# Placing the sign of a float64 weight with the scaling instruction on ScalarE instead of a bitwise instruction on VectorE

## The chip, the cores and the metric

The kernel runs on one core of a Trainium2 chip. The metric is the device time of one execution in microseconds (us); three runs of the kernel before gave 1048.39, 1048.4 and 1048.1, median 1048.39. The engines are named as in the profile: PE (TensorE matrix products), PEld (its weight loads), DVE (VectorE), ACT (ScalarE), POOL (GpSimd) and SP (SyncE, which issues all DMAs here; SPq is its queue).

## The reference

Three parts run one after the other on 2304 rows. The weights (`moe_w_*`, `moe2_w_*`) arrive as float64, everything else as float32.

```python
# q, k, v: (4, 8, 576, 64); average over groups of 4 rows, full attention on the averages
out_up = repeat(softmax(scale * q_d @ k_d.T) @ v_d, 4)
# banded attention: key within 3 rows of the query
out_local = softmax(where(|i - j| < 4, scale * q @ k.T, -1e9)) @ v
x = (out_up + out_local)                      # -> (2304, 512)
x = (silu(x @ w_gate) * (x @ w_val)) @ w_out  # 512 -> 1536 -> 512
h = x @ w_in                                  # 512 -> 2048
return (max(h, 0) + alpha * min(h, 0)) @ w_out2
```

## The kernel before

**Products.** Each float32 operand is held as a high and a low part, and each product is three PE instructions (high*high, high*low, low*high: lines 464 to 466 and 601 to 603). So each weight has to be turned from float64 into two such parts before PE can use it.

**Weights.** The five weight matrices are cut into 68 pieces. `w_load` (lines 99 to 108) brings a piece into a slot as raw 32-bit word pairs, 128 partitions by 512 weights (512 KB). `w_split` (lines 121 to 134) turns it into the two parts, which then take the slot:

- line 126, ACT: the high word, read as a float32, times 2^-112, into a working tile `st`;
- line 127, DVE: `st` shifted left by 3 bits;
- line 128, DVE: the sign bit of the high word is masked out and OR-ed into `st`;
- line 130, DVE: the top 3 bits of the low word are OR-ed into `st`, which is now the float32 weight;
- line 133, ACT: the high part, a rounded copy;
- line 134, POOL (DVE for half of the 32 pieces of the last part): the low part, `st` minus the high part.

36 pieces (lines 493 to 495, `prep1`) belong to the gated layer and are split at the start; 32 (lines 554 to 556, `prep2`) belong to the last layer and are split while the gated layer's last block and the last layer's first block run.

**Stages.** The attention of the first two 288-row blocks (8 head pairs) runs first, its tiles lying in slots that later weights take, so that the loads of these weights wait for it. Then the gated layer runs over 8 blocks of 288 rows by 12 pieces of 128 hidden columns (functions `m_g`, `m_v`, `m_y`: gate product, value product, output product), with the attention of the later blocks spread between them. Block 0 needs pieces 0 to 11 of each of the three matrices, and splits them as it goes. The last layer (`m2_h`, `m2_o`) runs over 5 blocks by 16 pieces.

**Order.** The program is written for a tiling framework that adds the semaphores and lets a planner with its own simulated costs and times decide in which order each engine's instructions are issued; a cost that changes can thus move other instructions in the queues. A few splits at the start are held behind attention steps on POOL by hand (`gP` in line 19, lines 485 to 491).

Of the kernel before, what the change touches and what calls it, by code (L numbers as in the profile page):

```python
# [8 lines left out]
F32 = mybir.dt.float32  # L9
F32R = mybir.dt.float32r  # L10
I32 = mybir.dt.int32
AF = mybir.ActivationFunctionType
ALU = mybir.AluOpType
AX = mybir.AxisListType
PSUM = bass.MemoryType.PSUM
DRAM = bass.MemoryType.DRAM
# [6 lines left out]
def attn_moe_moe2_kernel(  # L23
# [13 lines left out]
    nc = tc.nc  # L37
    B, H, S, D = q.shape
# [19 lines left out]
    scale = 1.0 / float(D) ** 0.5  # L58
    NEG = -1.0e9 / scale

# [1 line left out]
    wp = ctx.enter_context(tc.tile_pool(name="wp", bufs=1))  # L62
    dp = ctx.enter_context(tc.tile_pool(name="dp", bufs=1, space=DRAM))
    pp = ctx.enter_context(tc.tile_pool(name="pp", bufs=1, space=PSUM))
# [9 lines left out]
    mask = wp.tile([128, 4, SWIN], F32, name="mask")  # L74
# [7 lines left out]
    def f32(t):  # L82
        return t.bitcast(F32)

# [1 line left out]
    # A float64 word pair (H, L) becomes float32 bits: H * 2^-112 rebases the exponent, << 3 aligns it,  # L86
    # the sign comes from H and the last three mantissa bits from L. The float32 is then split exactly
    # into a 12-bit high part and a 12-bit low part.
    wsrc = {"g": w_gate.bitcast(I32), "v": w_val.bitcast(I32), "o": w_out.bitcast(I32),
            "i2": w2_in.bitcast(I32), "o2": w2_out.bitcast(I32)}  # L90

# [20 lines left out]
    def st_tile():  # L112
        c = stc[0]
        stc[0] += 1
        if c >= 3 * NEARLY:
            return stp[0].tile([128, 512], F32, tag="st", name="st", bufs=stn[0])
        if c % 2 == 0:
            stc[1] = wp.tile([128, 2, 512], F32, tag=st_slots[c // 2 % len(st_slots)], name="st2")
        return stc[1][:, c % 2]

    def w_split(slot, eng):
        t = raw.pop(slot)
        st = st_tile()
        sti = st.bitcast(I32)
        hw, lw = t[:, :, 1], t[:, :, 0]
        nc.scalar.mul(out=st, in_=hw.bitcast(F32), mul=2.0 ** -112)
        nc.vector.tensor_scalar(out=sti, in0=sti, scalar1=3, scalar2=None, op0=ALU.logical_shift_left)
        nc.vector.scalar_tensor_tensor(out=sti, in0=hw, scalar=-2 ** 31, in1=sti,  # L128
                                       op0=ALU.bitwise_and, op1=ALU.bitwise_or)
        nc.vector.scalar_tensor_tensor(out=sti, in0=lw, scalar=29, in1=sti,  # L130
                                       op0=ALU.logical_shift_right, op1=ALU.bitwise_or)
        w = W[slot] = wp.tile([128, 2, 512], F32R, tag=slot, name="w")
        nc.scalar.copy(out=w[:, 0], in_=st)  # L133
        eng.tensor_sub(w[:, 1], st, f32(w[:, 0]))  # L134

# [1 line left out]
    hu = {}  # L137
    kTs = {}
    pbd = {}
# [5 lines left out]
    def coords(n):  # L145
        blk, hp = divmod(n, NP)
        b, half = divmod(blk, 2)
        return b, half, hp, blk
# [11 lines left out]
    def at_(n, shape, tag):  # L160
        return wp.tile(shape, F32, tag=pslot[tag, n], name=tag)

    def small(n):
        # working tiles of one head pair: parts of a weight slot at first, the pool's after that
        d = hu[n]
        if n < NPRO:
            t = at_(n, [128, 1024], "qs")
            d["qT"] = t[:, 0:HB + 8]
            d["pt"] = t[:72, 0:4 * QD].rearrange("p (h x) -> p h x", h=2)
            o = HB + 8  # L170
            d["sm"] = t[:, o:o + 2 * SW].rearrange("p (h x) -> p h x", h=2)
            d["xf"] = t[:, o:o + HB]
            o += 2 * SW
            d["qd"] = t[:, o:o + QD]
            d["up"] = t[:, o + QD:o + 2 * QD]
        else:
            d["qT"] = ap_.tile([128, HB + 8], F32, tag="qT", name="qT", bufs=1)
            d["qd"] = ap_.tile([128, QD], F32, tag="qd", name="qd", bufs=1)
# [6 lines left out]
    def a_load(n):  # L185
        b, half, hp, blk = coords(n)
        h0, t0 = 2 * hp, half * HB
        d = hu[n] = {}
        if n >= NPRO:
            # 32 x 32 blocks for the transposing copy: partition 32 i + r, column 32 m + c is row 32 m + r, column 32 i + c  # L190
            loads = [("qn", q, HB, t0)]
            if half == 0:
                loads.insert(0, ("kn", k, S, 0))
            for tag, src, rn, r0 in loads:
                t = d[tag] = ap_.tile([128, rn], F32, tag=tag, name=tag, bufs=1)
                for i in range(4):
                    nc.sync.dma_start(
                        out=t[32 * i:32 * (i + 1)].rearrange("r (m c) -> r m c", c=32),
                        in_=src[b, h0 + i // 2, r0:r0 + rn, 32 * (i % 2):32 * (i % 2 + 1)].rearrange("(m r) c -> r m c", r=32))
            return  # L200
        if half == 0:
            kn = d["kn"] = at_(n, [QB, 6, 2, D], "kn")
            for h in range(2):
                nc.sync.dma_start(out=kn[:, :, h], in_=k[b, h0 + h].rearrange("(r p) c -> p r c", p=QB))
        t = at_(n, [128, 2 * NW * 2 * D], "qv").rearrange("p (a w h c) -> p a w h c", a=2, w=NW, h=2)
        d["vw"] = t[:, 1]
        qn = d["qn"] = t[:QB, 0]
        for h in range(2):
            nc.sync.dma_start(out=qn[:, :, h], in_=q[b, h0 + h, t0:t0 + HB, :].rearrange("(r p) c -> p r c", p=QB))
# [16 lines left out]
                nc.sync.dma_start(out=vf, in_=v[b, h0:h0 + 2, f * HB:(f + 1) * HB].rearrange("h (p r) c -> p h (r c)", r=4))  # L226

    def a_load_w(n):
        # v rows of the 32-key window of each 24-query tile; rows outside the sequence meet a zero weight
        b, half, hp, blk = coords(n)  # L230
        if n < NP:
            pbd[n] = at_(n, [128, 2, NW, 128], "bd")
            (nc.vector if K["bdV"] else nc.gpsimd).memset(pbd[n], 0.0)
        if n >= NPRO:
            hu[n]["vw"] = ap_.tile([128, NW, 2, D], F32, tag="vw", name="vw", bufs=NVW)
        t = hu[n]["vw"]
        for h in range(2):
            w0 = ((b * H + 2 * hp + h) * 2 + half) * NW * 128
            nc.sync.dma_start(out=t[:, :, h], in_=vwin[w0:w0 + NW * 128, :].rearrange("(w p) c -> p w c", p=128))

    def stage(b):
        # DRAM copy of v in overlapping windows: window g holds rows 24 g - 3 .. 24 g + 28; rows outside v meet a zero weight
        nw = H * S // SUB
        g0, g1, ng = b * nw, (b + 1) * nw, B * nw

        def win(a, e):
            n = (e - a) * SWIN
            nc.sync.dma_start(
                out=vwin[a * SWIN:e * SWIN, :].rearrange("(g r) c -> g (r c)", r=SWIN),
                in_=bass.AP(v.tensor, v.offset + (a * SUB - 3) * D, [[SUB * D, e - a], [1, SWIN * D]]))  # L250

        vf = v.rearrange("b h s c -> (b h s) c")
        if g0 == 0:
            nc.sync.dma_start(out=vwin[0:3, :], in_=vf[0:3, :])
            nc.sync.dma_start(out=vwin[3:SWIN, :], in_=vf[0:SWIN - 3, :])
            win(1, 16)
            g0 = 16
        if g1 == ng:
            win(g0, g1 - 16)
            win(g1 - 16, g1 - 1)  # L260
            r0, m = (g1 - 1) * SWIN, SUB + 3
            nc.sync.dma_start(out=vwin[r0:r0 + m, :], in_=vf[B * H * S - m:, :])
            nc.sync.dma_start(out=vwin[r0 + m:r0 + SWIN, :], in_=vf[0:SWIN - m, :])
        else:
            win(g0, g1)
# [193 lines left out]
                        hp_.tile([128, KD, HB], F32R, tag="xl", name="xl"))  # L459
        return xts[blk]  # L460

# [1 line left out]
    def mm3(o, lhi, llo, rhi, rlo, first, last):  # L463
        nc.tensor.matmul(o, lhi, rhi, start=first, stop=False)  # L464
        nc.tensor.matmul(o, lhi, rlo, start=False, stop=False)  # L465
        nc.tensor.matmul(o, llo, rhi, start=False, stop=last)  # L466
# [10 lines left out]
    gates = {}  # L477

    def gate(n, stage):
        # the last instruction traced so far on each engine  # L480
        bb = tc.nc.cur_bb.bb.instructions
        for key, eng in (("D", nc.vector), ("P", nc.gpsimd), ("A", nc.scalar)):
            gates[key, n, stage] = next(i for i in reversed(bb) if i.engine == eng.engine)
# [51 lines left out]
                    out=y1[e * 128:(e + n) * 128, blk * HB:(blk + 1) * HB].rearrange("(e p) t -> p e t", p=128),  # L535
                    in_=ys.unsqueeze(1) if n == 1 else ys)

# [1 line left out]
    blocks2 = [512, 512, 512, 512, 256]  # L539
    starts2 = [sum(blocks2[:i]) for i in range(len(blocks2))]  # L540
    HT = []
# [75 lines left out]
        r0 = starts2[i] + m * 128  # L617
        nc.sync.dma_start(out=out[r0:r0 + 128, :], in_=os_)

# [1 line left out]
    if True:  # L621
        make_identity(nc, ident)
        for tok in K["lo"]:
# [11 lines left out]
        for t in srs:  # L635
            nc.vector.memset(t, 1.0)

        # mask[32 i + r, :, j]: key window j of query r of tile i; 0 <= j - r <= 6, cut at both ends of the sequence
        tmp = ap_.tile([SWIN, 4, NS, SWIN], F32, tag="vd", name="tmp", bufs=NVD)
        nc.gpsimd.memset(tmp, 0.0)  # L640
        nc.gpsimd.affine_select(out=tmp, in_=tmp, pattern=[[0, 4], [0, NS], [1, SWIN]], compare_op=ALU.is_ge, fill=NEG,
# [90 lines left out]
        for n in range(NPRO, NHU):  # L732
            if n < 2 * NP:
                c = K["c"]
# [56 lines left out]
        for t in range(len(f2s)):  # L791
            if True:
                i, j = f2s[t]
# [8 lines left out]
            if SK <= t < len(f2s):  # L802
                i, j = f2s[t - SK]
# [32 lines left out]
```

## Time and profile before

| | |
|---|---|
| time, median of 3 runs | 1048.39 us (1048.1 to 1048.4) |
| profiled execution, first to last instruction (span) | 1047.0 us |
| profiled execution's own time | not listed apart from its span; the median lies 1.4 us above the span |
| PE busy | 978.3 us (93%) |
| DVE busy | 557.9 us (53%) |
| POOL busy | 401.7 us (38%) |
| ACT busy | 292.2 us (28%) |

These are shares of the whole span. The page also cuts the span into 40 slices of 26 us; PE's digits there are 5368779 followed by nines, and DVE's are 4899997 at the start, 4 to 6 in the middle, 99972 behind it and 2 to 3 to the end. The stages therefore differ, and are read apart: the rows below come from the stretches 28 to 172 us (the 36 splits of the gated layer), 172 to 580 us, 580 to 700 us (the 32 splits of the last layer) and 700 us to the end.

### The profile page before, as it was taken

Reading aid. Unit: us, or ns where it says so; the run is one execution under the profiler, and the core shown is the slowest. Engines: PE = TensorE matmul, PEld = TensorE weight load, DVE = VectorE, ACT = ScalarE, POOL = GpSimd, SP = SyncE. Lnnn points to the kernel's source line nnn. Section 1 sums busy time; section 2 is a strip of 40 time slices with the busy share of each in tenths; the row PEclk is TensorE's granted clock in tenths of the full one; section 3 lists DMA queues with packets and bytes.
Section 4 is the critical chain, followed back from the end, with each engine's and each line's share of the span. In section 5 each row is a group of like instructions: output and inputs, shape, how many; then the busy total and the mean of one; then the engine's idle time right before and its main releaser. Section 6 shows DMA issues by size and latency. Waiting matters only on the chain.

```text
span 1047.0 us, 19294 instructions
## 1 busy us (share of the span) xinstructions
PE 978.3 (93%) x7760; PEld 872.4 (83%) x7760; DVE 557.9 (53%) x1113; ACT 292.2 (28%) x660; POOL 401.7 (38%) x492
## 2 busy tenths in 40 slices
PE   5368779999999999999999999999999999999998
PEld 4257668999999999999999998778888888888887
DVE  4899997546544555545451699972222322232232
ACT  3545443222222222222223445432111201111111
POOL 5666676223432234322224344653222322322222
PEclk9989879999999999999999999999999999999999
DMA  8995463114221132111101884200100200010010
GB/s 207 282 308 185 122 146 82 28 26 89 47 58 19 35 72 49 26 45 21 44 17 41 263 261 154 72 1 20 61 1 1 71 1 1 11 41 0 1 41 21
DMA packets 135895, 77.82 MB, mean 74 GB/s; under 512 B 97407, under 2 KB 127103, under 8 KB 135039
## 3 DMA queue, kind: packets, MB, share of 16 engines
q1 hardware_dynamic: 135804, 76.58, 26.4%
q8 instruction: 61, 1.00, 0.4%
q14 instruction: 30, 0.24, 0.1%
HBM read 67.12 MB, written 15.73 MB: 79 GB/s over the span
## 4 chain that ended last, share of the span: by engine, by line
PE 72%; DVE 12%; SPq 5%; DMA 3%; issue 3%; POOL 2%; ACT 2%; DVEq 0%; ACTq 0%; POOLq 0%
PE y L603 6%; PE y L601 6%; PE y L602 6%; PE g L464 5%; PE v L465 5%; PE v L464 5%; PE g L465 5%; PE g L466 5%; PE v L466 5%; PE y L464 4%; PE y L466 4%; PE y L465 4%; DVE st L128 3%; PE h L464 3%; PE h L466 3%
## 5 line engine op out<-in xcount | busy, mean ns | idle before, releaser
L589 POOL TENSOR_TENSOR gl<-t,gh 128x512 fp32r<-128x512 f32 (+1 forms) x80 | 97.1, 1215 | 253.5 <-ACT gh L588 228.5
L464 PE MATMUL g<-xh,w 128*128 128x288 f32 x384 | 118.6, 309 | 12.9 <-DVE u L504 7.2
L464 PE MATMUL v<-xh,w 128*128 128x288 f32 x384 | 117.4, 306 | 9.5 <-DVE u L510 7.0
L588 ACT CAST gh<-t 128x512 fp32r<-128x512 f32 (+1 forms) x80 | 46.2, 578 | 269.3 <-DVE t L585 224.7
L504 DVE SCALAR_TENSOR_TENSOR u<-u,g 128x288 f32<-128x288 f32 x96 | 43.3, 451 | 142.1 <-ACT u L503 142.1
L466 PE MATMUL g<-xh,w 128*128 128x288 f32 x384 | 115.6, 301 | 2.5 <-POOL w L134 2.5
L466 PE MATMUL v<-xh,w 128*128 128x288 f32 x384 | 115.4, 300 | 1.4 <-POOL w L134 1.4
L465 PE MATMUL v<-xl,w 128*128 128x288 f32 x384 | 116.6, 304 | 0.0
L465 PE MATMUL g<-xl,w 128*128 128x288 f32 x384 | 115.8, 302 | 0.0
L465 PE MATMUL y<-pl,w 128*128 128x288 f32 x384 | 114.6, 301 | 1.1 <-POOL pl L514 1.1
L466 PE MATMUL y<-ph,w 128*128 128x288 f32 x384 | 114.0, 299 | 0.0
L601 PE MATMUL y<-w,gh 128*128 128x512 f32 x288 | 113.2, 393 | 0.8 <-ACT sy L533 0.8
L603 PE MATMUL y<-w,gl 128*128 128x512 f32 x288 | 112.3, 394 | 1.8 <-POOL gl L589 1.8
L602 PE MATMUL y<-w,gh 128*128 128x512 f32 x288 | 112.8, 392 | 0.0
L464 PE MATMUL y<-ph,w 128*128 128x288 f32 x384 | 112.0, 304 | 0.0
L514 POOL TENSOR_TENSOR pl<-u,ph 128x288 fp32r<-128x288 f32 x96 | 84.2, 877 | 63.5 <-ACT ph L513 63.1
L134 POOL TENSOR_TENSOR w<-st,w 128x512 fp32r<-128x512 f32 x52 | 77.7, 1498 | 61.2 <-ACT w L133 58.6
L464 PEld LDWEIGHTS g<-xh,w 128*128 128x128 f32 x384 | 74.2, 193 | 16.9 <-DVE u L504 9.8
L583 DVE TENSOR_SCALAR t<-h,alpha 128x512 f32<-128x512 f32 (+1 forms) x40 | 27.9, 696 | 103.6 <-PE h L466 101.3
L464 PEld LDWEIGHTS v<-xh,w 128*128 128x128 f32 x384 | 73.8, 192 | 11.0 <-DVE u L510 4.0
L466 PEld LDWEIGHTS g<-xh,w 128*128 128x128 f32 x384 | 74.4, 194 | 2.9 <-POOL w L134 2.9
L466 PEld LDWEIGHTS v<-xh,w 128*128 128x128 f32 x384 | 74.2, 193 | 2.1 <-POOL w L134 2.0
(189 smaller groups left out, 2193.2 us busy)
## 6 DMA issues: line engine op xcount, KB each, us to landing
raw<-in_moe_w_out_dram SPq DMA_DIRECT2D x28, 512.0 KB
raw<-in_moe_w_in_dram SPq DMA_DIRECT2D x16, 512.0 KB
raw<-in_moe_w_gate_dram SPq DMA_DIRECT2D x12, 512.0 KB
raw<-in_moe_w_val_dram SPq DMA_DIRECT2D x12, 512.0 KB
vw<-vwin SPq DMA_DIRECT2D x48, 96.0 KB
out_dram<-os SPq DMA_DIRECT2D x18, 256.0 KB
sy<-y SPq DMA_DIRECT2D x16, 256.0 KB
y<-ys SPq DMA_DIRECT2D x14, 288.0 KB
```

Source lines behind the costliest of these rows:

```text
L128: nc.vector.scalar_tensor_tensor(out=sti, in0=hw, scalar=-2 ** 31, in1=sti, op0=ALU.bitwise_and, op1=ALU.bitwise_or)
L134: eng.tensor_sub(w[:, 1], st, f32(w[:, 0]))
L464: nc.tensor.matmul(o, lhi, rhi, start=first, stop=False)
L465: nc.tensor.matmul(o, lhi, rlo, start=False, stop=False)
L466: nc.tensor.matmul(o, llo, rhi, start=False, stop=last)
L504: nc.vector.scalar_tensor_tensor(out=u, in0=u, scalar=1.0, in1=GV[0][:, :HB], op0=ALU.add, op1=ALU.mult)
L514: nc.gpsimd.tensor_sub(pl, u, f32(ph))
L588: nc.scalar.copy(out=gh[:, :n], in_=t[:, :n])
L589: nc.gpsimd.tensor_sub(gl[:, :n], t[:, :n], f32(gh[:, :n]))
L601: nc.tensor.matmul(o, gh[:, ms], ohi, start=(j == 0), stop=False)
L602: nc.tensor.matmul(o, gh[:, ms], olo, start=False, stop=False)
L603: nc.tensor.matmul(o, gl[:, ms], ohi, start=False, stop=(j == F2 - 1))
```

## The change

The scaling in line 126 becomes a parametric ReLU: x * 2^-112 where that is positive, and -2^32 times it where it is negative. For a negative weight the result is a positive number whose exponent is larger by 32; that bit of the exponent field lies 3 places below the sign bit, so the left shift by 3 of line 127 puts it into the sign's place. The masking instruction of line 128 falls away, and `w_split` has two DVE instructions ahead of the rounded copy instead of three. The rest of the diff takes comment lines out.

```diff
-        nc.scalar.mul(out=st, in_=hw.bitcast(F32), mul=2.0 ** -112)
+        nc.scalar.activation(out=st, in_=hw.bitcast(F32), func=AF.Prelu, scale=2.0 ** -112, alpha=-2.0 ** 32)
         nc.vector.tensor_scalar(out=sti, in0=sti, scalar1=3, scalar2=None, op0=ALU.logical_shift_left)
-        nc.vector.scalar_tensor_tensor(out=sti, in0=hw, scalar=-2 ** 31, in1=sti,
-                                       op0=ALU.bitwise_and, op1=ALU.bitwise_or)
         nc.vector.scalar_tensor_tensor(out=sti, in0=lw, scalar=29, in1=sti,
                                        op0=ALU.logical_shift_right, op1=ALU.bitwise_or)
```

## Rows read from the trace of the kernel before

**Rows 1.** Stretches: length; busy PE, PEld, DVE, ACT, POOL (instructions); PE clock, DMA share, GB/s
```profile
28.00:85.00 57.00, 30.85 (x394) 26.98 (x395) 54.97 (x110) 30.17 (x81) 34.79 (x46) 0.94 0.88 270
28.00:172.00 144.00, 99.06 (x967) 89.55 (x968) 141.72 (x249) 70.06 (x165) 99.31 (x104) 0.89 0.67 194
172.00:580.00 408.00, 408.00 (x4298) 388.78 (x4297) 195.89 (x517) 105.00 (x275) 130.34 (x219) 1.00 0.19 43
580.00:700.00 120.00, 113.59 (x653) 99.37 (x652) 110.12 (x155) 57.37 (x106) 59.61 (x41) 1.00 0.52 161
700.00:1047.00 347.00, 342.40 (x1585) 283.52 (x1583) 97.39 (x149) 51.46 (x92) 96.15 (x84) 1.00 0.06 20
```

**Rows 2.** What PE waited for, 28 to 172 us (total us, times, longest)
```profile
PE v L464 <- DVE u L510: 7.0, 4, 3.1
PE g L464 <- DVE qs L446: 5.5, 1, 5.5
```

**Rows 3.** DVE's costliest groups, 28 to 172 us (count, busy us, mean ns, idle)
```profile
L130 DVE SCALAR_TENSOR_TENSOR st<-raw,st 128x512 int32<-128x512 int32 x36 | 36.1, 1005 | 0.1
L128 DVE SCALAR_TENSOR_TENSOR st<-raw,st 128x512 int32<-128x512 int32 x36 | 32.7, 908 | 0.1
L127 DVE TENSOR_SCALAR st<-st 128x512 int32<-128x512 int32 x36 | 26.7, 746 | 7.8 <-ACT st L126 7.8
```

**Rows 4.** Timeline of DVE, then of POOL, around 140 and 149 us (start, us)
```profile
142.92 0.68 DVE L128 SCALAR_TENSOR_TENSOR st<-raw,st 128x512 int32<-128x512 int32 x1
143.52 0.41 DVE L127 TENSOR_SCALAR st<-st 128x512 int32<-128x512 int32 x1
143.85 0.68 DVE L128 SCALAR_TENSOR_TENSOR st<-raw,st 128x512 int32<-128x512 int32 x1
149.13 1.81 DVE L130 SCALAR_TENSOR_TENSOR st<-raw,st 128x512 int32<-128x512 int32 x1
...
141.71 3.19 POOL L362 TENSOR_TENSOR sm<-sm,mx 128x192 f32<-128x192 f32 x1
149.12 1.27 POOL L134 TENSOR_TENSOR w<-st,w 128x512 fp32r<-128x512 f32 x1
```

**Rows 5.** POOL's group of line 134, 28 to 172 us (count, busy us, mean ns, idle)
```profile
L134 POOL TENSOR_TENSOR w<-st,w 128x512 fp32r<-128x512 f32 x36 | 52.1, 1451 | 30.0 <-ACT w L133 27.3 <-DMA qv<-vwin 2.4
```

**Rows 6.** ACT's groups, 28 to 172 us (count, busy us, mean ns, idle)
```profile
L126 ACT ACTIVATE st<-raw 128x512 f32<-128x512 f32 x36 | 23.7, 670 | 14.8 <-DMA raw<-in_moe_w_gate_dram 6.6 <-POOL w L134 6.4 <-DMA raw<-in_moe_w_out_dram 1.3
L133 ACT CAST w<-st 128x512 fp32r<-128x512 f32 x36 | 22.2, 618 | 42.3 <-DVE st L130 38.8 <-DVE sr L391 2.1 <-DVE qs L446 1.4
L503 ACT ACTIVATE u<-g 128x288 f32<-128x288 f32 x13 | 5.3, 405 | 1.2 <-PE g L466 1.2
L379 ACT ACTIVATE qs<-qs 128x192 f32<-128x192 f32 x6 | 2.1, 359 | 2.0 <-POOL qs L362 2.0
L381 ACT ACTIVATE sm<-sm 72x288 f32<-72x288 f32 x2 | 0.9, 445 | 2.7 <-DVE sm L359 2.7
...
L370 ACT ACTIVATION_READ_ACCUMULATOR qs<-y,nb 72x1 f32 x4 | 0.8, 194 | 0.0
```

**Rows 7.** Two groups of DVE, 580 to 700 us, and PE's waits there
```profile
L128 DVE SCALAR_TENSOR_TENSOR st<-raw,st 128x512 int32<-128x512 int32 x32 | 29.5, 922 | 0.5
L504 DVE SCALAR_TENSOR_TENSOR u<-u,g 128x288 f32<-128x288 f32 x11 | 4.9, 447 | 0.0
...
PE g L464 <- DVE u L504: 3.8, 6, 1.1
PE y L603 <- POOL gl L589: 1.8, 3, 0.7
```

**Rows 8.** The longest wait of SP's queue, 0 to 200 us
```profile
SPq L103 <- PE att L441: 34.8, 2, 25.5
```

**Rows 9.** The table load of ACT (count, shortest/median/longest ns, first and last start)
```profile
L291 ACT ACT_TABLE_LOAD  x1: 1283/1283/1283, 6.5 to 6.5; - x1
```

**Rows 10.** Instructions on tile st, 85 to 172 us (length; DVE, ACT, POOL busy; clock, DMA)
```profile
85.00:172.00 87.00, 58.27 (x68) 28.06 (x45) 34.21 (x23) 0.86 0.54 144
```

## The prediction

> **What bounds the kernel now.** I read the 40 slices of the page first, because an average over the span hides that only two places leave PE idle. Busy time by stretch then gives sizes [rows 1]: PE is busy for all 408 us between 172 and 580, so nothing that DVE does there can matter, and it is busy for 342.4 of the last 347 us. It is idle for 144.0 - 99.1 = 44.9 us between 28 and 172, and for 120.0 - 113.6 = 6.4 us between 580 and 700. These two stretches are the ones in which weights are split. In the first DVE is busy for 141.7 of 144 us, the next engine (POOL) for 99.3, ACT for 70.1, and the DMA engines for 0.67 of the time. The reader should see a queue that never empties. Next come the waits: the longest of PE's own name a DVE result, 7.0 and 5.5 us in all, with no stall above 5.5 [rows 2], which is how a saturated engine looks from PE. Last I read DVE's groups there [rows 3]: three instructions of the weight split fill 36.1 + 32.7 + 26.7 = 95.5 of the 141.7 us, and line 128, which goes, is 32.7 of them.
>
> **The change part by part.**
>
> *What goes in the first stretch.* 36 instructions of line 128. Their mean is 908 ns, but that is not what an empty place in the queue saves. Two neighbours in the timeline show the free pace: one starts at 142.92 and its successor at 143.52, so 0.60 us where nothing blocks it [rows 4]. The excess, 36 x (0.908 - 0.60) = 11.1 us, is made of about 0.08 us of overlap with the next instruction each (0.68 against 0.60: 2.9 us) and of 8.2 us of blocking. What blocks is visible at 149: POOL starts line 134 at 149.12 and takes 1.27 us, DVE starts line 130 at 149.13 and takes 1.81 us, as if it began when POOL was done (1.27 + 0.60 = 1.87). The reverse happens at 141.71, where a POOL instruction of line 362 lasts 3.19 us while DVE issues its split instructions one after the other [rows 4]. So the two engines take turns at something. If POOL's 36 subtractions meet whichever split instruction comes next, the 8.2 us pass to lines 127 and 130 and are not saved. Bounds: 36 x 0.60 = 21.6 us if all blocking stays, 32.7 us if all of it goes. I take 21.6, since the two engines together have no room: POOL's 99.3 us and three split instructions at free pace (0.60 + 0.60, and 0.33 for line 127 from 143.52 to 143.85 [rows 4]), 36 x 1.53 = 55.1 us, make 154.4 in 144 us, so either engine's release is taken up at once by the other.
>
> The Trainium skill says the same more sharply (SBUF — State Buffer, "Who interferes with whom"): a VectorE instruction with two SBUF inputs and a GpSimd instruction that reads SBUF exclude each other for a whole instruction. By that rule the first stretch saves 21.6 us, and by a mean that is taken as the instruction's own price it would save 32.7 us.
>
> *What stays in the path.* The removed time is worth its length as long as DVE, or DVE with POOL, still ends last. Without line 128 DVE has 141.7 - 21.6 = 120.1 us of work in the stretch, which is more than POOL's 99.3, PE's 99.1, ACT's 70.1 and the DMA engines' 0.67 x 144 = 96.5 [rows 1]. So the stretch should end about 22 us earlier, and whatever follows is PE-bound and moves with it. The loads that wait up to 25.5 us at a time for the attention's last products [rows 8] move too, because these products stand behind DVE work.
>
> *What is changed on ACT.* The scaling of 128x512 takes 670 ns, a rounded copy of the same size 618 ns [rows 6]. The parametric ReLU is an instruction of the same engine and shape that appears in no row. From below I bound it by the copy's 618; from above by the scaling plus one small follow-up instruction such as the 194 ns of an accumulator read, 864 ns. I take 670, as the nearest row. At the upper end 36 x 0.194 = 7.0 us are added to an engine with 144 - 70 = 74 us free, and the cover is DVE's longer queue; at 618 ns, 1.9 us go from it. Either way the sum gets 0, unless the chain of one split counts, and that chain loses a 0.60 us step, more than the 0.19.
>
> *Waits and queues.* No wait is added and no DMA moves by the edit itself. Line 127 waits for ACT as before, and line 130 stays the last reader of the raw words, so the slot comes free as before, only earlier. The planner recomputes the order from its own costs; I have no row for that and put 0, with a rival below.
>
> *The second stretch.* 32 instructions go, 32 x 0.60 = 19.2 us of DVE at least, 29.5 us at most [rows 7]. DVE's 110.1 of 120 us become about 91, and PE's 113.6 us become the bound. So the gain is limited by PE's idle time, 6.4 us [rows 1]. The waits there that name DVE or the POOL work behind it are 3.8 + 1.8 = 5.6 us [rows 7]. I take 5.
>
> *Sum.* 21.6 + 5 = 26.6 us against the profiled execution's span of 1047.0 gives 1020.4. The median of the runs lies 1.4 us above that span, so the forecast is 1021.8 us. Its own range, if only sizes are off: a third of the first term lost to the holes of a queue that is no longer full (-7 us) to half of the blocking gained (+4) and all 6.4 of the second: 1016 to 1029.
>
> **Rivals.**
>
> *The loads take over early.* The DMA engines are at a share of 0.88 and 270 GB/s between 28 and 85 us [rows 1], and ACT's scaling waited 6.6 + 1.3 us for weights [rows 6]. If the splits there can't go faster than the loads, only the 23 splits after 85 us gain (68 DVE instructions on their tile, three to a split [rows 10]): 23 x 0.60 = 13.8, with the 5 of the second stretch 18.8, so 1029.6 us. Against it: DVE was idle for only 2 of those 57 us, so the loads ran ahead of it.
>
> *The whole mean goes.* If the blocking vanishes with the instruction and PE's holes in the second stretch all close: 32.7 + 6.4 = 39.1, so 1009.3 us. For it: POOL waits 27.3 us for the copy of line 133, which waits 38.8 us for line 130 [rows 5, 6], and a shorter chain shifts POOL's work to where it meets less. Against it: the sum of 154.4 in 144 us above.
>
> *Table loads on ACT (slower).* All of ACT's functions so far run on one table load, 1.283 us at the start [rows 9]. If the parametric ReLU needs another table than Exp and Tanh, each change between them costs a load. Among the 36 splits ACT runs 13 Tanh of line 503 and 20 Exp in six groups, the first of 6 (line 379), the last of 2 (line 381) [rows 6], so up to 33 pairs of changes, 66 loads, 84.7 us. ACT then has 70.1 + 84.7 = 154.8 us in a stretch of 144, and becomes the bound; it decides from (144 - 70.1) / 1.283 = 58 loads. The stretch would be 10.8 us longer; in the second, 11 Tanh, one for each instruction of line 504 [rows 7], give 22 loads, 28 us on top of ACT's 57.4 in 120, which I let eat the 5 us gain: 1059.2 us. Against it: copies, casts and scalings already share the table with Exp and Tanh, and a function with two straight lines is the same sort of thing.
>
> The Trainium skill (ScalarE: Activation LUTs, "Table sets: the hidden batching unit") says that cheap functions, relu among them, are in every set, which speaks against this rival, but its list does not name a parametric ReLU; by the same page's estimate of about 2.7 us for each switch, loads and drains together, the 66 switches would cost some 176 us on ACT and the time would lie near 1150 us. No run here shows it.
>
> *The planner's new order gives it back.* The simulated times change, and the order of attention steps against splits on POOL and PE with them; if attention ends as late as before, the loads behind it [rows 8] do so too, and the time stays within 1046 to 1050. Nothing in the trace speaks for this except that the order is computed.
>
> **How the numbers follow.** Forecast 0.56; loads take over 0.20; whole mean 0.12; table loads 0.06; planner 0.06. The predicted time is the forecast's, 1021.8. The range takes in the forecast's own, the loads' rival with room for fewer gaining splits or a lost second stretch (1029.6 + 6) and the whole mean's 1009.3: 1008 to 1036. About 0.2% (2 us) is what a measurement can tell from no change. Faster by more than that: the first three and a third of the planner's, 0.90; within it: 0.03; slower: the table's and the rest, 0.07.
>
> **What would show it.** In the changed profile line 128's group (now a gap) must be gone with DVE at about 250 - 36 instructions up to the point where PE turns steadily busy, which should come near 150 us instead of 172. Lines 127 and 130 should have higher means than 746 and 1005 ns if blocking stays, and lower ones if the whole mean went. PE between there and the last layer should stay without holes. The Prelu's mean should be about 670 ns with one table load in all. If DVE is well below 95% busy while the DMA share is near 1 before 80 us, the loads took over. The forecast is wrong in its root if PE's idle time in the first stretch stays near 45 us though DVE lost 36 instructions.

## The result and the profile after

The changed kernel takes 1023.48 us (median of 4 runs, 1022.0 to 1024.78) against 1048.39; the ratio is 0.9765, with a 95% interval of 0.9751 to 0.9778. The forecast was 1021.8 us with a range of 1008 to 1036. The profiled execution has a span of 1020.1 us and took 1022.0.

Busy time by stretch in the changed kernel (columns as in [rows 1]); the third row ends where the output of block 0 is stored, the last begins where that of block 6 is:

```profile
28.00:85.00 57.00, 39.20 (x508) 34.75 (x509) 52.50 (x108) 34.55 (x90) 40.04 (x53) 1.00 0.97 304
28.00:172.00 144.00, 114.99 (x1189) 105.11 (x1190) 120.97 (x241) 76.29 (x181) 102.88 (x119) 0.96 0.69 204
28.00:151.00 123.00, 94.70 (x985) 86.02 (x986) 111.61 (x217) 71.41 (x169) 94.03 (x105) 0.96 0.77 226
150.90:219.00 68.10, 67.39 (x722) 63.82 (x722) 33.99 (x89) 16.27 (x43) 20.85 (x38) 1.00 0.20 44
558.30:1020.10 461.80, 453.68 (x2233) 382.94 (x2232) 177.47 (x271) 108.68 (x197) 147.65 (x124) 1.00 0.18 57
```

The same stretches of the kernel before, ended by the same stores:

```profile
28.00:176.00 148.00, 103.06 (x1016) 93.33 (x1017) 144.18 (x255) 71.19 (x168) 102.79 (x109) 0.90 0.66 189
176.70:241.20 64.50, 64.50 (x685) 61.23 (x685) 32.53 (x86) 16.04 (x42) 17.99 (x33) 1.00 0.20 40
580.60:1047.00 466.40, 455.39 (x2233) 382.29 (x2231) 207.51 (x303) 108.28 (x196) 155.30 (x124) 1.00 0.18 56
```

DVE does 217 instructions up to the end of block 0 where it did 255 (36 of the 38 are line 128), and 32.6 us less work (144.18 - 111.61). It is no longer full: 11.4 of 123 us are idle, against 3.8 of 148. Block 1 takes 68.1 us where it took 64.5, with 37 more PE instructions (722 against 685): 20 attention products and 17 gate and value products, which lay ahead of block 0's end before. From block 6 on, 461.8 us replace 466.4.

DVE's groups up to the end of block 0 (columns as in [rows 3], the former line 130 is now line 128):

```profile
L128 DVE SCALAR_TENSOR_TENSOR st<-raw,st 128x512 int32<-128x512 int32 x36 | 35.1, 979 | 0.6
L127 DVE TENSOR_SCALAR st<-st 128x512 int32<-128x512 int32 x36 | 27.5, 766 | 10.5 <-ACT st L126 10.2
```

The two take 62.6 us, where three took 95.5 [rows 3]: 32.9 us are gone, the whole of line 128's 32.7 and not the 21.6 of its free pace. (Of the idle 10.5 us before line 127, 7.9 are one wait that ends at 29 us; the kernel before has it too, with 7.8.) What PE waits for in the first stretch has also changed (28 to 150 us, columns as in [rows 2]); the 7.0 us for the value product are gone, and the largest sum is now seven short waits:

```profile
PE g L462 <- DVE u L502: 7.4, 7, 2.1
PE att L439 <- DMA qv<-vwin: 5.5, 1, 5.5
PE g L462 <- DVE qs L444: 3.6, 1, 3.6
```

The second of these, for a load of the windows of v, stood in the kernel before with the same length, between the two of [rows 2]; the change did not touch it:

```profile
PE att L441 <- DMA qv<-vwin: 5.5, 1, 5.5
```

On ACT, the new instruction (shortest, median, longest ns over the whole span) and the table load:

```profile
L126 ACT ACTIVATE st<-raw x68: 657/672/692, 28.5 to 651.0; 128x512 f32<-128x512 f32 x68
...
L289 ACT ACT_TABLE_LOAD  x1: 1283/1283/1283, 6.6 to 6.6; - x1
```

Its median is 672 ns, where the scaling had a mean of 670 [rows 6], and there is still one table load [rows 9].

### The profile page after: what moved, and what is told of

Same layout as the page of the kernel before. It is cut to its first block, busy times and chain, and to the rows that moved or that the text cites. A ratio compares the mean times of both kernels' runs of the same rounds, so it can differ in the third digit from the quotient of the medians.

```text
span 1020.1 us, 19253 instructions
## 1 busy us (share of the span) xinstructions
PE 970.3 (95%) x7760; PEld 867.5 (85%) x7760; DVE 496.7 (49%) x1045; ACT 292.3 (29%) x660; POOL 387.7 (38%) x492
## 4 chain that ended last, share of the span: by engine, by line
PE 79%; DVE 7%; DMA 6%; SPq 4%; issue 2%; POOL 2%; ACT 1%; DVEq 0%; POOLq 0%; ACTq 0%
PE y L599 6%; PE y L601 6%; PE y L600 6%; PE g L462 6%; PE v L463 6%; PE v L462 5%; PE g L464 5%; PE g L463 5%; PE v L464 5%; PE y L462 4%; PE y L464 4%; PE y L463 4%; PE h L462 3%; PE h L464 3%; PE h L463 3%
## 5 line engine op out<-in xcount | busy, mean ns | idle before, releaser
L462 PE MATMUL g<-xh,w 128*128 128x288 f32 x384 | 117.0, 305 | 13.4 <-DVE u L502 8.8
L464 PE MATMUL g<-xh,w 128*128 128x288 f32 x384 | 114.6, 298 | 1.2 <-POOL w L132 1.2
L502 DVE SCALAR_TENSOR_TENSOR u<-u,g 128x288 f32<-128x288 f32 x96 | 43.3, 451 | 144.2 <-ACT u L501 144.1
L512 POOL TENSOR_TENSOR pl<-u,ph 128x288 fp32r<-128x288 f32 x96 | 80.8, 842 | 56.0 <-ACT ph L511 55.7
L132 POOL TENSOR_TENSOR w<-st,w 128x512 fp32r<-128x512 f32 x52 | 73.8, 1425 | 59.5 <-ACT w L131 57.8
L462 PEld LDWEIGHTS g<-xh,w 128*128 128x128 f32 x384 | 73.2, 191 | 16.8 <-DVE u L502 10.8
L463 PEld LDWEIGHTS y<-pl,w 128*128 128x128 f32 x384 | 72.4, 189 | 4.4 <-POOL pl L512 3.9
L462 PEld LDWEIGHTS y<-ph,w 128*128 128x128 f32 x384 | 71.0, 189 | 5.1 <-issue 4.2
L463 PEld LDWEIGHTS v<-xl,w 128*128 128x128 f32 x384 | 73.5, 191 | 1.7
```

The costliest lines, as they stand in the source:

```text
L502: nc.vector.scalar_tensor_tensor(out=u, in0=u, scalar=1.0, in1=GV[0][:, :HB], op0=ALU.add, op1=ALU.mult)
L512: nc.gpsimd.tensor_sub(pl, u, f32(ph))
```

## The experiments

All times are medians, each against runs of the kernel before on the same chip (1048.1 to 1048.8). For reading where a kernel gains, this table has three marks of each profiled execution: the first store of block 0's output (the DMA of `y` from `ys`), that of block 1's, that of block 6's, and what is left from there to the end, in us. Six kernels whose first stretch has the same issue order (changed, e2, e3, e7, e10, e11) end block 0 between 150.6 and 152.9, so a mark is good to some 2 us; the rests of kernels that are alike there agree within 0.6.

| kernel | time | block 0 | block 1 | block 6 | rest |
|---|---|---|---|---|---|
| before | 1048.39 | 176.67 | 241.21 | 580.57 | 466.4 |
| changed | 1023.48 | 150.89 | 219.00 | 558.35 | 461.8 |
| e1 new ACT instruction, line 128 kept | 1048.02 | 177.00 | 241.55 | 580.93 | 466.0 |
| e2 old ACT instruction, line 128 gone | 1022.54 | 151.73 | 219.46 | 558.84 | 461.4 |
| e3 first 36 splits only | 1027.84 | 152.36 | 220.03 | 559.40 | 466.6 |
| e4 last 32 splits only | 1043.36 | 175.15 | 239.70 | 579.08 | 460.4 |
| e5 reduction in its place, scratch column | 1027.59 | 169.97 | 235.00 | 574.42 | 453.9 |
| e8 reduction in its place, no column | 1028.1 | 163.79 | 228.34 | 567.72 | 457.9 |
| e6 copies of v later | 1025.64 | 154.40 | 220.59 | 559.97 | 462.5 |
| v1 a third of the low parts on DVE | 1025.47 | 158.57 | 223.57 | 562.96 | 461.7 |
| e7 changed, scratch column | 1019.27 | 152.86 | 220.41 | 559.82 | 457.6 |
| e9 before, scratch column | 1044.68 | 176.16 | 240.71 | 580.12 | 462.5 |
| e10 reduction in the last 32 splits | 1018.48 | 150.56 | 217.92 | 557.30 | 457.9 |
| e11 e10 and the scratch column | 1015.33 | 152.54 | 220.23 | 559.65 | 453.5 |

**The two halves of the edit.** e1 puts the new ACT instruction in and keeps line 128; e2 takes line 128 out and keeps the old one, so that the sign is left out.

```diff
# e1, against before
-        nc.scalar.mul(out=st, in_=hw.bitcast(F32), mul=2.0 ** -112)
+        nc.scalar.activation(out=st, in_=hw.bitcast(F32), func=AF.Prelu, scale=2.0 ** -112, alpha=-2.0 ** 32)
# e2, against before
-        nc.vector.scalar_tensor_tensor(out=sti, in0=hw, scalar=-2 ** 31, in1=sti,
-                                       op0=ALU.bitwise_and, op1=ALU.bitwise_or)
```

> The parametric ReLU on ACT, and line 128 kept behind it (it masks and ORs a sign that is already in place). Every engine gets its instructions in the order of the kernel before. Theory (the parametric ReLU costs ACT what the scaling costs, and all the gain is line 128's): the time of the kernel before, 1048.4 us within 2, about 670 ns for the new instruction and one table load. Rival (part of the gain or of a loss lies in the ACT instruction, by another table or another duration): a time off 1048.4 by more than 2 us, and more than one table load or a mean off 670 ns by over 50.

> The plain scaling kept and line 128 left out, so the weights lose their sign: that part of the computation is left out. Order of instructions as in the changed kernel. Theory: the time of the changed kernel, 1023.5 us within 2. Rival (the parametric ReLU itself matters): off by more than 2 us.

e1: 1048.02 us, ratio 0.9987 (0.9976 to 0.9999). e2: 1022.54, ratio 0.9747 (0.9730 to 0.9765). The issue order on every engine was that of the kernel before for e1 and that of the changed kernel for e2, so nothing but the instruction differs. ACT's instruction in e1, and its table load:

```profile
L126 ACT ACTIVATE st<-raw x68: 647/675/703, 28.4 to 693.8; 128x512 f32<-128x512 f32 x68
...
L291 ACT ACT_TABLE_LOAD  x1: 1283/1283/1283, 6.5 to 6.5; - x1
```

The parametric ReLU costs what the scaling costs and shares the table with Exp and Tanh. All the gain is line 128's, the order included that the planner draws up without it.

e1 also answers a rival that the prediction does not name, TensorE's clock. PE's granted clock up to the end of block 0 has a mean of 0.90 in the kernel before and 0.96 in the changed one. In e1 it was 0.93, and block 0 ended within 0.4 us of the kernel before; so a higher mean of half that size does not by itself move this end:

```profile
28.00:177.00 149.00, 101.25 (x1021) 90.47 (x1022) 144.38 (x255) 71.74 (x170) 101.20 (x110) 0.93 0.65 190
```

**The two stretches.** The change for the first 36 splits, or for the last 32:

```diff
+        new = stc[0] <= 3 * F1   # e3; e4: stc[0] > 3 * F1
... (if new: the Prelu without line 128; else: the scaling with line 128)
```

> The change for the 36 splits of the gated layer alone; the 32 of the last layer as before. Theory (two separate gains, about 22 us in the first stretch and 5 in the second): 1048.4 - 22 = 1026 to 1029 us. Rival (the second stretch, where the planner put the splits earlier, brings more than its 5 us, or the first gain is given back in it): above 1032 or at the changed kernel's 1023.5.

> The change for the 32 splits of the last layer alone. Theory: 1048.4 - 5 = 1043 to 1044 us, PE's idle time between 580 and 700 us falling from 6.4 to under 2. Rival (the second stretch is bound by something else, such as the loads or POOL): within 2 us of 1048.4.

e3: 1027.84 us, ratio 0.9797 (0.9776 to 0.9817), so 21.0 us less than the 1048.82 of its chip's runs. e4: 1043.36, ratio 0.9949 (0.9933 to 0.9965), 5.5 less. Together 26.5, within 1.6 us of the changed kernel's whole gain of 24.9. The marks put e3's gain before block 1's store and e4's behind block 6's, with 460.4 us left there instead of 466.4. The two theories of the expectations hold in size and place.

**What line 128 gave up: free time or turn-taking?** e5 puts another DVE instruction into line 128's place, a maximum over the row. It has about the same length but reads one SBUF operand instead of two.

```diff
         nc.vector.tensor_scalar(out=sti, in0=sti, scalar1=3, scalar2=None, op0=ALU.logical_shift_left)
+        nc.vector.tensor_reduce(out=scr, in_=st, axis=AX.X, op=ALU.max)
...
+    scr = wp.tile([128, 1], F32, name="scr")   # further up
```

> The changed kernel with a VectorE instruction of about line 128's own length in its old place: a maximum over the 512 values of st into one scratch column. It reads one SBUF operand, and 128x512 of its kind should take about 0.66 us (the reductions 128x576 take 0.74 us in the trace). Theory (the free time in DVE's queue is what the change gave): the gain goes, except for the blocking by POOL that line 128 met, 8 us of DVE time in the first stretch: 1038 to 1048 us. Rival (what counted was the turn-taking with POOL, in which a one-operand instruction has no part): near the changed kernel, under 1032 us. DVE's mean of lines 127 and 128 (the former 130) then tells whether blocking is passed on: 766 and 979 ns in the changed kernel's first stretch.

At 1027.59 us (ratio 0.9802, 0.9783 to 0.9821) the rival's number came out. The marks say something else: block 0 ends at 170, much nearer to the kernel before, and it is the rest that is 12.5 us shorter than there. (The profiled execution, 1030.81 us, was the slowest of the four, and the planner drew up an order for e5 that no other kernel here has, so its block 0 is a rough figure.) Part of that is the pace of the products of 512 columns, whose rows below differ in count for the same 200 us of a busy PE, from 250 us before the end on, first in the changed kernel and then in e5:

```profile
770.10:970.10 200.00, 200.00 (x884) 163.85 (x883) 54.13 (x77) 28.85 (x49) 55.28 (x45) 1.00 0.05 16
```

```profile
778.30:978.30 200.00, 200.00 (x895) 166.04 (x894) 55.23 (x78) 28.80 (x49) 55.25 (x45) 1.00 0.05 16
```

e8 takes the scratch column out by letting the reduction write a word of the raw piece that nobody reads any more.

```diff
+        nc.vector.tensor_reduce(out=t[:, 0:1, 1].bitcast(F32), in_=st, axis=AX.X, op=ALU.max)
```

> The reduction in line 128's place once more, now with its result put into a word of the raw piece that nobody reads any more, so that no scratch column is added and every tile lies where it lies in the changed kernel. In the kernel with the scratch column, products of 512 columns in the last layer were spaced 0.227 us instead of 0.233, which hid what the reduction costs. Theory (free time in DVE's queue is the gain, and the scratch column's place in SBUF sped up the last layer): block 0 ends near 170 us as there, the spacing is 0.233 again, and the time is 1034 to 1042 us. Rival (the time is that of turn-taking with POOL, and the scratch column does nothing): 1026 to 1030 us.

e8: 1028.1 us, ratio 0.9814 (0.9795 to 0.9832), with 881 products in 200 us, the old pace. The theory's 1034 to 1042 is wrong, and the rival's number came out: with an instruction of 0.67 us still in line 128's place, 20 of the 25 us are gained. Block 0 ends at 163.79, halfway between the two kernels (12.9 us from either), and the rest is 3.9 us shorter than in the changed kernel. In e8 every engine issues its instructions in the order of the kernel before, with the reduction where line 128 was (on PE a few neighbours that start within 0.6 us are swapped in the trace), so against that kernel only this instruction and the Prelu, which by e1 costs nothing, differ. Up to 164 us, for DVE's groups up to 161 us, and the reduction's shortest, median and longest ns:

```profile
28.00:164.00 136.00, 97.94 (x1023) 88.09 (x1024) 130.76 (x255) 71.99 (x170) 94.90 (x108) 0.94 0.71 206
```

```profile
L129 DVE SCALAR_TENSOR_TENSOR st<-raw,st 128x512 int32<-128x512 int32 x36 | 35.5, 989 | 0.1
L127 DVE TENSOR_SCALAR st<-st 128x512 int32<-128x512 int32 x36 | 24.4, 684 | 8.1 <-ACT st L126 8.1
L128 DVE TENSOR_REDUCE raw<-st 128x1 f32<-128x512 f32 x36 | 24.2, 672 | 0.1
...
L128 DVE TENSOR_REDUCE raw<-st x36: 626/672/687, 30.4 to 154.5; 128x1 f32<-128x512 f32 x36
```

Two places show what happens when POOL is at its subtraction (start, us), in the kernel before and then in e8:

```profile
62.15 1.34 POOL L134 TENSOR_TENSOR w<-st,w 128x512 fp32r<-128x512 f32 x1 [1.28 <-ACT w L133]
62.27 1.76 DVE L128 SCALAR_TENSOR_TENSOR st<-raw,st 128x512 int32<-128x512 int32 x1
...
132.40 1.28 POOL L133 TENSOR_TENSOR w<-st,w 128x512 fp32r<-128x512 f32 x1 [1.35 <-ACT w L132]
132.47 0.67 DVE L128 TENSOR_REDUCE raw<-st 128x1 f32<-128x512 f32 x1
```

DVE again does 255 instructions, and they take 130.8 us instead of 144.2; POOL's 108 take 94.9 us, where 109 took 102.8. Counted from the trace of the kernel before, the 9 instructions of line 128 that ran while POOL did nothing took 679 ns on average, the 27 that ran beside a POOL instruction 985. The 36 reductions took 672 to 673 ns either way (27 of them beside POOL). Lines 127 and 130 are not slower in e8 than before (684 and 989 against 746 and 1005 [rows 3]), so the waiting was not handed on to them.

So line 128 cost this stretch in two ways. Its meeting with POOL cost 11.4 us in DVE's three lines (95.5 - 84.1), and taking that away moves the ends of blocks 0 and 1 by 12.9 us: this is shown, since the order is the same. Its own time, some 21.5 us (84.1 - 62.6), brings another 12.9 us at block 0's end and 9.3 at block 1's; in this second step the planner's order changes too, and no run separates the two. From block 6 on, the first step alone brings 8.5 us (466.4 to 457.9), and the changed kernel, with less DVE work but its new order, loses 3.9 of them again.

What spares the reduction is not separated either: it reads one SBUF operand, but it also writes one value where line 128 writes 512. That it reads one operand is not enough as a reason: line 127 reads one as well, and in the kernel before it took 416 ns on average without POOL at work and 841 beside it.

**Do the loads or POOL bound the changed kernel?** e6 issues 6 MB of DRAM copies behind a later weight load; v1 moves 12 of the 36 subtractions of line 132 from POOL to DVE.

```diff
-                            with tc.issue_after(wdma[f"o{F1 - 1}"]):   # e6
+                            with tc.issue_after(wdma[f"v{F1 - 1}"]):
-K = dict(... lo1=0, ...)                                               # v1
+K = dict(... lo1=1, ...)
```

> The changed kernel with the copies of v for the third and fourth batch (DRAM to DRAM, some 6 MB read and written) issued behind the load of the last value piece instead of behind that of the last output piece, so they no longer run among the weight loads at 56 to 75 us. Theory (in the changed kernel the loads now hold part of DVE up: it is idle for 11 of 123 us up to the end of block 0, against 4 of 148 before): 2 to 6 us less, 1017 to 1021. Rival (DVE's idle time comes from dependencies behind 85 us, not from loads): within 2 us of 1023.5, or slower if the copies now delay the later loads.

> The changed kernel with the low parts of the output pieces' splits in the first stretch (12 of 36) computed on DVE instead of POOL. Theory (DVE's queue still bounds the first stretch): 12 x 0.60 = 7.2 us more on DVE against the blocking by 12 POOL instructions that goes, up to 23 x 12/36 = 7.7 us: within 4 us of 1023.5. Rival (POOL is the bound now, with 93 of 122 us and its own waits): 4 us or more faster.

e6: 1025.64 us, ratio 0.9778 (0.9763 to 0.9792). My theory that the loads now hold DVE up is not borne out: the time is no shorter, block 0 ends 3.5 us later, and DVE is idle for as long as in the changed kernel (126.4 - 115.2 = 11.2 us up to there), though the DMA share between 28 and 85 us fell from 0.97 to 0.81:

```profile
28.00:85.00 57.00, 35.10 (x440) 30.75 (x441) 54.88 (x111) 36.90 (x94) 42.70 (x53) 1.00 0.81 244
```

v1: 1025.47, ratio 0.9769 (0.9751 to 0.9787), the theory's "within 4 us". POOL has 13 us less to do up to the end of block 0 (81.4 us in 130.6, against 94.0 in 123) and the block ends 7.7 us later, so nothing here points to POOL alone as the bound. For both kernels the planner drew up an order of its own, so neither test is clean. What makes up DVE's 11 idle us stays open; behind 30 us it lies in waits of at most 1.4 us each, mostly for ACT, PE and POOL.

**The scratch column.** One float32 for each partition, allocated ahead of the weight slots and set to zero once; it does nothing but move what is allocated behind it.

```diff
+    scr = wp.tile([128, 1], F32, name="scr")
+    nc.vector.memset(scr, 0.0)
```

> The changed kernel with nothing added but the scratch column (one float32 for each partition, set to zero once), which moves the tiles behind it in SBUF. Theory (the place of the tiles sets the spacing of the 512-column products): spacing 0.227 us and, with some 1500 such products, 7 to 10 us less: 1013 to 1017 us. Rival (the spacing came from the planner's order with the reduction): 0.233 us and 1023.5 us within 2.

> The kernel before with the same scratch column. Theory (place of the tiles): 7 to 10 us less than before, 1038 to 1042 us, so the column and the change add up. Rival (the planner's order): 1048.4 us within 2.

e7: 1019.27 us, ratio 0.9725 (0.9710 to 0.9741). e9: 1044.68, ratio 0.9966 (0.9957 to 0.9976). The issue order on every engine is that of the kernel without the column. Both gain about 4 us, half of what I expected: I had taken the changed kernel's widest spacing, 0.233 us, for its mean, which the counts put at 200 / 884 = 0.226 against 200 / 895 = 0.223. The direction holds in both kernels, and nearly the whole gain of e9 lies in the rest (462.5 against 466.4). Counted from the traces, the last 1300 products of 512 columns take 320.62 us in every kernel here without the column and 317.76 in each of the four with it, whatever the order. The 12.5 us by which e5's rest is shorter than before are thus about e8's 8.5 and e9's 3.9. In 200 us, e7 and then e9:

```profile
767.40:967.40 200.00, 200.00 (x895) 166.16 (x894) 55.29 (x79) 28.80 (x49) 55.23 (x45) 1.00 0.05 16
```

```profile
792.60:992.60 200.00, 200.00 (x894) 165.99 (x893) 55.21 (x78) 28.80 (x49) 55.36 (x46) 1.00 0.05 16
```

**A version that beats both.** e8's rest was shorter than the changed kernel's though DVE had 32 instructions more in it. e10 therefore puts its reduction into the last 32 splits alone, e11 adds the scratch column.

```diff
+        if stc[0] > 3 * F1:
+            nc.vector.tensor_reduce(out=t[:, 0:1, 1].bitcast(F32), in_=st, axis=AX.X, op=ALU.max)
```

> The changed kernel, with the reduction (result into the raw piece, no scratch column) put in for the 32 splits of the last layer alone. From the end of block 6 to the end, the kernel with the reduction in all splits took 457.9 us against 461.8 in the changed one and 466.4 before, although VectorE had more to do. Theory (the planner's order, not VectorE's load, decides what is left in that stretch): block 0 ends near 151 us as in the changed kernel, and the rest from the end of block 6 takes 458: some 4 us less, 1018 to 1021 us. Rival (that stretch depends on where the first one ended): 1023.5 us within 2, or slower by the reductions.

> The same with the scratch column, whose place alone gave 4 us. Theory (the two add up): 1014 to 1017 us, faster than all kernels so far. Rival: no faster than the changed kernel with the scratch column, 1019.3 us within 2.

e10: 1018.48 us, ratio 0.9716 (0.9697 to 0.9734). e11: 1015.33, ratio 0.9681 (0.9665 to 0.9697), the fastest kernel here. Both times came out as the theory had it. Its reason, the planner's order, is only part of it: in e10 every engine's issue order is that of e3, which is the kernel before's from block 6 on, and with line 128 in those 32 splits e3 takes 466.6 us there. So in one and the same order the instruction that does not wait for POOL saves 8.7 us; the changed kernel, with no instruction in that place, has another order there. From block 6 on, e10:

```profile
557.70:1015.20 457.50, 452.09 (x2230) 382.35 (x2228) 196.22 (x303) 107.75 (x196) 148.93 (x123) 1.00 0.18 57
```

DVE is busy for 196 us in it, 19 more than in the changed kernel, and PE is idle for 5.4 us instead of 8.1. How the splits lie shows in the timeline of ACT's scalings (start, us), of the changed kernel, then of e10 and of e3, in the same stretch behind the end of block 6:

```profile
570.79 0.69 ACT L126 ACTIVATE st<-raw 128x512 f32<-128x512 f32 x1 [0.31 <-DMA raw<-in_moe_w_in_dram]
572.07 0.66 ACT L126 ACTIVATE st<-raw 128x512 f32<-128x512 f32 x1 [0.29 <-DMA raw<-in_moe_w_out_dram]
575.58 0.67 ACT L126 ACTIVATE st<-raw 128x512 f32<-128x512 f32 x1
576.88 0.67 ACT L126 ACTIVATE st<-raw 128x512 f32<-128x512 f32 x1 [0.63 <-DMA raw<-in_moe_w_out_dram]
580.91 0.67 ACT L126 ACTIVATE st<-raw 128x512 f32<-128x512 f32 x1 [0.70 <-DMA raw<-in_moe_w_in_dram]
```

```profile
570.86 0.69 ACT L126 ACTIVATE st<-raw 128x512 f32<-128x512 f32 x1 [1.53 <-DVE w L134]
573.75 0.69 ACT L126 ACTIVATE st<-raw 128x512 f32<-128x512 f32 x1
576.58 0.68 ACT L126 ACTIVATE st<-raw 128x512 f32<-128x512 f32 x1 [1.32 <-DVE w L134]
579.21 0.67 ACT L126 ACTIVATE st<-raw 128x512 f32<-128x512 f32 x1 [0.54 <-POOL w L134]
```

```profile
573.57 0.70 ACT L130 ACTIVATE st<-raw 128x512 f32<-128x512 f32 x1 [1.66 <-DVE w L139]
576.88 0.68 ACT L130 ACTIVATE st<-raw 128x512 f32<-128x512 f32 x1 [0.36 <-POOL w L139]
579.71 0.68 ACT L130 ACTIVATE st<-raw 128x512 f32<-128x512 f32 x1 [1.33 <-DVE w L139]
```

The changed kernel's come in pairs, 1.3 us apart and then 3.5 to 4.0, and mostly wait for loads; e10's come every 2.6 to 2.9 us and wait for a working tile. In e3 they come nearly as evenly, every 2.8 to 3.3 us in these rows, and its stretch is the longest of the three, so an even spacing alone does not bring the gain. Why the changed kernel's order costs it some 4 us there is not shown.

## Why the prediction was right

- *The first stretch ends about 22 us earlier.* Right in sum: 25.8 us at block 0's end and 22.2 at block 1's, 21.0 in e3.
- *"If POOL's 36 subtractions meet whichever split instruction comes next, the 8.2 us pass to lines 127 and 130."* This step failed. The waiting for POOL left with line 128: e8, which keeps an instruction of the same length that POOL does not hold up, in the same order, ends block 0 12.9 us earlier than before. The excess of the means over the free pace (0.60 and 0.33 us, 0.08 of overlap each) was 95.5 - 55.1 - 8.6 = 31.8 us for three lines in the kernel before, and is 62.6 - 33.5 - 5.8 = 23.3 for two in the changed one; the 8.5 between them are line 128's own share. The sum of 154.4 us of work in 144, from which I took it that the blocking stays, did not decide it.
- *"The removed time is worth its length as long as DVE ... still ends last."* Only partly, and this made up for the step above: of 32.6 us of DVE work 7.6 came back as idle time of DVE (11.4 against 3.8) up to block 0's end, and 3.6 of the 25.8 us went back in block 1. The forecast's 21.6 thus came out by luck, on two errors that cancel: a saving too small by 11 and a loss of 11 left out. By the marks at block 1 the 22.2 us are 12.9 of waiting, which I had put at 0, and 9.3 of line 128's own time, which I had put at 21.6.
- *POOL and DVE take turns.* Borne out: line 128 took 985 ns beside POOL and 679 without, and in e8 255 instructions take 13.4 us less. The rule of the Trainium skill (SBUF — State Buffer, "Who interferes with whom"), that a VectorE instruction with two SBUF inputs and a GpSimd instruction that reads SBUF exclude each other, agrees with this; its "fully blocks" does not say that the waiting is handed on, which I had read into it. That line 127, with one input, is held up too (841 against 416 ns) the rule as I quoted it does not cover.
- *ACT gets 0, no table load.* Right: 672 ns, one load, and e1 at 1048.02 us. The rival of the tables is out.
- *The second stretch gives 5 us, limited by PE's idle time.* Right in size: 4.6 by the marks, 5.5 in e4. But 6.4 us was not the limit: e10's rest is 8.5 us shorter than the kernel before's, and e11's 12.9, some 4 of which are the column's.
- *The loads take over early.* Not borne out: e6 is no faster. But the DMA share did rise to 0.97 between 28 and 85 us, in which PE is still idle for 17.8.
- *The planner's new order gives it back.* In part, from block 6 on: in the old order e8 and e10 take 457.9 us there with 32 more DVE instructions, the changed kernel in its new one 461.8. In the first stretch no run has the old order without an instruction in line 128's place, so this stays open.

## What to carry to other kernels

On a full engine, price an instruction's own time and its waits for a neighbour apart: here the waits brought 12.9 of the first 22.2 us, while the own time brought less than half its length. A queue that was 97% full did not stay full when a fifth of it went. A sum that comes out right is not proof of its terms; marks along the program (here the stores of the blocks) show which terms cancelled. Where a planner orders the instructions, put a dummy of the removed length back before calling the time its price, and compare the issue orders of the traces: the dummy here brought the old order back, which made the comparison clean.

## What the runs showed that I had not expected

- A bitwise DVE instruction of 128x512 with two SBUF operands took 985 ns on average beside a POOL instruction and 679 without one; a reduction of 128x512 took 672 to 673 ns either way, with a spread of 626 to 687.
- Four bytes for each partition, allocated ahead of the weight slots, make the same products of 512 columns, issued in the same order, follow each other at 0.223 instead of 0.226 us in the same 200 us before the end, with a granted clock of 1.00 in both: 2.9 us over the last 1300 of them, and some 4 us of time in both kernels. Which tile's place does it was not tried.
- An instruction that computes nothing of use, put into 32 splits, made the changed kernel 5 us faster: with it the planner issues them in the order of the kernel before.
